# Attention in two heads at a time: row-tiled score products in place of stacked ones, padded blocks of v, one chain for the decays

## The chip, the cores and the metric

The kernel runs on 1 core of one Trainium2 chip. A time is device microseconds (us) of that core for one execution. The kernel before takes 1095.51 us, the median of 3 runs (1094.81 to 1099.94).

## The reference

32 heads (4 batches of 8) of 576 positions by 64 features go through an attention with a forgetting decay, and what comes out, 2304 tokens of 512 features, goes through two feed-forward blocks. All is float32.

```
scores = scale * q @ k.T                     # scale = 1/8
cum    = cumsum(log(clip(f, 1e-4, 1)))       # along the 576 positions of a head
scores = where(causal, -1e9, scores + cum[:, None] - cum[None, :])
attn   = softmax(scores);  out = attn @ v
h = x @ w_in;    y = (max(h, 0) + log1p(exp(-abs(h)))) @ w_out
z = ((1 / (1 + exp(-(y @ w_gate)))) * (y @ w_val)) @ w2_out
```

## The kernel before, in words

Matrix products are made of float32r operands (one pass through TensorE, with fewer bits than float32). To keep the precision every operand is split in a high part (the value cast to float32r) and a low part (the rest), and a product is high·high + high·low + low·high. Small pieces are multiplied in float32 instead, which stands in a trace as two MATMUL records for one instruction.

The attention works on 16 pairs of heads. The 576 queries of a head are four blocks of 128 and a rest of 64. A pair has nine score tiles, `t` = 0 to 3 (blocks of head 0), 4 (the rests of both heads in one tile of 128 rows) and 8 down to 5 (blocks of head 1), of the causal widths `W9`: 128, 256, 384, 512 and 576.

- `scores` (lines 236 to 265): `X` holds the high part of q on rows 0 to 63 and its low part on rows 64 to 127, `Y` the high part of k twice, so that one product over 128 rows (K = 128) makes two of the three terms. `X2` holds the high part of q again and two rows of ones, `Y2` the low part of k and the two rows of the decay, so that a second product with K = 66 makes the third term and the decay. That is two products a tile (line 262; line 251 for tile 4). The first block of a head (tiles 0 and 8) is made of a product with K = 2 for the decay (line 258, rows 64 and 65) and a float32 product with K = 64 (line 259). A score tile lies in PSUM under tag `s` (two buffers), tile 4 under tag `X`.
- `minimum` (VectorE, line 269) adds the causal mask, scales, writes the tile to SBUF (`P`) and finds the row's extreme; `exp` (ScalarE, line 274) follows.
- `transposes` (TensorE, line 291, 25 blocks of 128 by 128 a pair) put the tiles of `P` into PSUM tag `t` (two buffers); `evac_h` (ScalarE) and `evac_l` (VectorE, line 310) take the high and the low part out. The blocks listed as "f" in `GROUPS` stay float32 and are copied once (`evac_f`).
- `pv` multiplies with v: line 371 in float32r with the high and low parts of v side by side (128 columns of weights), line 367 in float32 for the "f" blocks, some of them with 64 columns of weights. The sums stand in PSUM tags `Y` (head 0) and `X` (head 1).
- `out_a` (ScalarE) and `out_b` (VectorE, line 386) add the two halves, `out_c` (GpSimd) divides by the row sums, `out_d` stores to `xT`.
- The splits of q, k and v into parts are casts and subtractions on GpSimd, VectorE and ScalarE (`copy` line 193 to 197, `sub` line 201).

The order of the work is written out: `run` sorts all operations of all pairs by 9·p + `WHEN[op]` (`START` for pair 0, `END` for pair 15), mixed with steps of the first feed-forward block (`TICKS`, `LATE_TICKS`, `X_STEPS`, `UNITS`), and every engine takes its instructions strictly in that order. Pairs overlap: while pair p makes scores, pair p-1 is transposed and multiplied with v. At the start `begin` follows the list `BEGIN`: clip, logarithm, running sum and the two parts of the decay are made first for head 0, then for head 1, then for all 32 heads (into `nb_d` in DRAM, from which later pairs fetch theirs). During and after the attention VectorE, ScalarE and GpSimd also unpack the weights of the feed-forward blocks; TensorE runs these blocks from about 227 us to the end. None of that code changes.

Of the kernel before, what the change touches and what calls it, by code (L numbers as in the profile page):

```python
# [21 lines left out]
class Attention:  # L22


    S = 576
# [10 lines left out]
    def pools(self, pool, io_pool):  # L36
# [10 lines left out]

    BEGIN = [["clip", 0], ["clip", 1], ["ones", 0], ["log", 0], ["scan", 0], ["m"], ["log", 1], ["mask4"],
             ["mask"], ["qh", 0, "A"], ["scan", 1], ["ql", 0, "P"], ["kh", 1, "A"], ["high", 0],
             ["kh", 0, "P"], ["high", 1], ["ahead"], ["kl", 0, "P"], ["kl", 1, "P"], ["clip", 2], ["log", 2],  # L50
             ["low", 1], ["ones", 1], ["qh", 1, "A"], ["low", 0], ["scan", 2], ["q2", 0, "A"], ["high", 2],
             ["ql", 1, "P"], ["low", 2], ["q2", 1, "A"]]

    def begin(self, ahead):

        nc, S = self.nc, self.S
        R = 2 * self.NP
        c = self.pp.tile([128, sum(self.W9)], F32, tag="P", name="decays")  # L60
        f0, cum0 = c[64:66, 0:2 * S], c[64:66, 2 * S:4 * S]
        fs, cums = [c[0:R, 0:S]], [c[0:R, S:2 * S]]
        nb = c[0:R, 2 * S:4 * S].rearrange("p (t s) -> p t s", t=2).bitcast(F32R)
        nc.sync.dma_start(f0, bass.AP(self.f.tensor, self.f.offset, [[0, 2], [1, 2 * S]]))
        P0 = self.R[0] = {}
        self.load_q(P0, 0)
        self.load_k(P0, 0)
        nc.sync.dma_start(fs[0], self.f)
        self.load_first(P0, 0)
        fs = [f0[:, 0:S], f0[:, S:]] + fs  # L70
        cums = [cum0[:, 0:S], cum0[:, S:]] + cums
        self.constants()
        X, X2, Y, Y2 = (self.buf(P0, 0, n) for n in ("X", "X2", "Y", "Y2"))
        qr, kr = P0["qr"], P0["kr"]
        m = self.c.tile([128, 1], F32, name="m")
        self.nb = self.dr.tile([R, 2, S], F32, name="nb_d")

        def op(n, h=0, e="V"):
            f, cum = fs[h], cums[h]
            h = min(h, 1)  # L80
            if n == "ahead":
                ahead()
            elif n == "m":
                nc.gpsimd.memset(m[64:66], 1.0)
                nc.gpsimd.memset(m[64:65], 0.0)
            elif n == "mask":
                nc.gpsimd.memset(self.mask, 0.0)
                nc.gpsimd.affine_select(self.mask, self.mask, pattern=[[-1, 512]], compare_op=ALU.is_ge,
                                        fill=-8e9, base=384, channel_multiplier=1)
            elif n == "mask4":  # L90
                nc.gpsimd.memset(self.mask4, 0.0)
                for i in range(2):
                    M = self.mask4[64 * i:64 * i + 64]
                    nc.gpsimd.affine_select(M, M, pattern=[[-1, S]], compare_op=ALU.is_ge, fill=-8e9, base=512,
                                            channel_multiplier=1)
            elif n == "ones":
                nc.gpsimd.memset(self.fix[h][64:96].bitcast(F32), 1.0)
            elif n == "clip":
                nc.vector.tensor_scalar(f, f, 1e-4, 1.0, op0=ALU.max, op1=ALU.min)
            elif n == "log":  # L100
                nc.scalar.activation(f, f, AF.Ln)
            elif n == "scan":
                nc.vector.tensor_tensor_scan(cum, f, f, 0.0, op0=ALU.add, op1=ALU.bypass)
            elif n == "high" and f is not fs[2]:
                nc.vector.tensor_scalar(f.bitcast(F32R), cum, -8.0, m[64:66], op0=ALU.mult, op1=ALU.mult)
            elif n == "high":
                nc.vector.tensor_scalar(nb[:, 0], cum, -8.0, None, op0=ALU.mult)
            elif n == "low" and f is not fs[2]:
                nc.vector.scalar_tensor_tensor(Y2[64:66, h], cum, -8.0, f, op0=ALU.mult, op1=ALU.subtract)
            elif n == "low":  # L110
                nc.vector.scalar_tensor_tensor(nb[:, 1], cum, -8.0, nb[:, 0], op0=ALU.mult, op1=ALU.subtract)
                nc.sync.dma_start(self.nb, nb.bitcast(F32))
            elif n == "qh":
                self.copy(None, X[0:64, h, 128:], qr[:, h, 128:], e)
            elif n == "ql":
                self.sub(None, X[64:128, h, 128:], qr[:, h, 128:], X[0:64, h, 128:], e)
            elif n == "q2":
                self.copy(None, X2[0:64, h, 128:], X[0:64, h, 128:], e)
            elif n == "kh":
                self.copy(None, Y[:, h], kr[:, h], e)  # L120
            elif n == "kl":
                self.sub(None, Y2[0:64, h], kr[0:64, h], Y[0:64, h], e)
        for o in self.BEGIN:
            op(*o)

    def constants(self):

        c, S = self.c, self.S
        self.mask = c.tile([128, 512], F32, name="mask")
        self.mask4 = c.tile([128, S], F32, name="mask4")  # L130
        self.fix = [c.tile([128, 2, S], F32R, name=f"X2_{i}") for i in range(2)]

    def constants2(self):
        nc, c = self.nc, self.c
# [6 lines left out]
        self.vr = [c.tile([128, 1024], F32, name=f"vr{i}") for i in range(self.NVR)]  # L141
        for t in self.vr:
            for o in (0, 192):
                nc.gpsimd.memset(t[:, o:o + 64], 0.0)
        self.pta = [[c.tile([128, 896], F32R, name=f"PTa{w}{i}") for w in "hl"] for i in range(2)]
        self.ptb = [c.tile([128, 1536], F32R, name=f"PTb{w}") for w in "hl"]
        self.ptf = [c.tile([128, 768], F32, name=f"PTf{i}") for i in range(2)]
# [3 lines left out]

    def load_q(self, R, p):
        b, hp = divmod(p, self.HP)
        R["qr"] = self.io.tile([64, 2, self.S], F32, tag="qr", bufs=1, name=f"qr{p}")
        self.nc.sync.dma_start(R["qr"], self.q[b, hp])

    def load_k(self, R, p):
        b, hp = divmod(p, self.HP)
        kr = R["kr"] = self.io.tile([128, 2, self.S], F32, tag="kr", bufs=1, name=f"kr{p}")
        for i in range(2):  # L160
            self.nc.sync.dma_start(kr[64 * i:64 * i + 64], self.k[b, hp])

    def load_first(self, R, p):

        b, hp = divmod(p, self.HP)
        for n, x in (("q0", self.q), ("k0", self.k)):
            R[n] = self.io.tile([64, 2, 128], F32, tag=n, name=f"{n}_{p}")
            self.nc.sync.dma_start(R[n], x[b, hp][:, :, 0:128])

    def load_v(self, R, p):  # L170
# [6 lines left out]
        else:  # L177
            nc.sync.dma_start(V[:, 0:4], rows[0:512].rearrange("(j p) e -> p j e", p=128))
            nc.sync.dma_start(V[0:64, 4], rows[512:576])

    def buf(self, R, p, n):
        if n == "X2":
            return self.fix[p % 2]
# [732 lines left out]
```

## Time and profile before

| | |
|---|---|
| median of 3 runs | 1095.51 us (1094.81 to 1099.94) |
| profiled execution | 1094.54 us, of which the span from the first to the last instruction is 1092.5 us |
| mean granted TensorE clock | 0.997 |
| TensorE (PE) | 1060.6 us busy, 97% of the span |
| VectorE (DVE) | 526.0 us, 48% |
| ScalarE (ACT) | 427.9 us, 39% |
| GpSimd (POOL) | 173.3 us, 16% |
| chain that ended last | PE 90%, DVE 5%, DMA 2%, ACT 1%, issue 1% |

A busy share is a mean over stages with different limits: the profile has to be read by stretches. A MATMUL record is longer than the time that it occupies TensorE, because matmuls are pipelined. What one costs is read from the start of one record to the start of the next. PEld are the loads of weights (the stationary operand), which run beside the matmul before them.

### The profile page before, as it was taken

The page shows a single profiled execution, that of the slowest core. Times are in us where ns is not written, and L with a number is a line of the kernel's source. Part 1 is how long each engine was busy: PE and PEld are TensorE (multiplying, and loading weights), DVE is VectorE, ACT ScalarE, POOL GpSimd, SP SyncE. Part 2 cuts the span into 40 slices and gives each one's busy share as a digit, 9 for nine tenths or more (in the row PEclk, how much of TensorE's full clock was granted, in tenths as well). Part 3 has the DMA queues.
Part 4 walks back from the last instruction along what each step waited for, and adds up shares of the span by engine and source line. Part 5 has one row for each costly group of instructions (what it writes and reads, how often), then busy time and mean ns, then how long its engine had stood idle before and what let it go on. Part 6 is the DMA issues. An engine that isn't in the chain of part 4 may idle for free.

```text
span 1092.5 us, 14676 instructions
## 1 busy us (share of the span) xinstructions
PE 1060.6 (97%) x5512; PEld 947.4 (87%) x5512; DVE 526.0 (48%) x1098; ACT 427.9 (39%) x930; POOL 173.3 (16%) x195
## 2 busy tenths in 40 slices
PE   3899999989999999999999999999999999999998
PEld 2777777767889999999999999999999999999997
DVE  8899989898971211212117879622222222222212
ACT  3788888865652222222225655311111111111111
POOL 7777777651000000000000000000000000000000
PEclk9999999999999999999999999999999999999999
DMA  6767766555531010010003544110010100100000
GB/s 184 180 161 185 187 173 163 153 156 173 210 143 56 17 36 15 18 43 9 17 35 119 181 167 171 53 42 17 1 44 16 37 15 8 37 15 8 30 1 29
DMA packets 52676, 90.26 MB, mean 83 GB/s; under 512 B 6704, under 2 KB 34304, under 8 KB 52606
## 3 DMA queue, kind: packets, MB, share of 16 engines
q1 hardware_dynamic: 52606, 89.33, 27.6%
q8 instruction: 43, 0.70, 0.3%
q14 instruction: 27, 0.22, 0.1%
HBM read 71.49 MB, written 14.38 MB: 79 GB/s over the span
## 4 chain that ended last, share of the span: by engine, by line
PE 90%; DVE 5%; DMA 2%; ACT 1%; issue 1%; SPq 0%; ACTq 0%
PE h L603 5%; PE h L604 5%; PE h L602 5%; PE pg L604 5%; PE pg L602 5%; PE pg L603 5%; PE pv L602 5%; PE pv L604 5%; PE pv L603 5%; PE t L291 4%; PE x L371 3%; PE s L262 3%; PE zX L753 3%; PE zX L752 3%; PE zX L751 3%; PE x L367 3%
## 5 line engine op out<-in xcount | busy, mean ns | idle before, releaser
L723 DVE TENSOR_TENSOR sg<-pv,sg 128x384 f32<-128x384 f32 x72 | 40.1, 557 | 262.0 <-PE pv L604 261.7
L644 DVE TENSOR_TENSOR gl<-L,gh 128x448 fp32r<-128x448 f32 (+1 forms) x80 | 51.0, 637 | 223.5 <-ACT gh L643 215.0
L632 ACT ACTIVATE L<-h 128x448 f32<-128x448 f32 (+1 forms) x80 | 44.3, 554 | 195.9 <-PE h L604 195.7
L603 PE MATMUL h<-xl,wi_h 128*128 128x448 f32 (+1 forms) x320 | 118.5, 370 | 1.0 <-POOL xl L595 1.0
L602 PE MATMUL h<-xh,wi_h 128*128 128x448 f32 (+1 forms) x320 | 118.7, 371 | 0.4 <-DVE xh L594 0.4
L604 PE MATMUL h<-xh,wi_l 128*128 128x448 f32 (+1 forms) x320 | 118.4, 370 | 0.0
L722 ACT ACTIVATE sg<-pg 128x384 f32<-128x384 f32 x72 | 35.3, 491 | 180.8 <-PE pg L604 180.8
L604 PE MATMUL pg<-yh,wg_l 128*128 128x384 f32 x288 | 97.1, 337 | 0.0
L602 PE MATMUL pg<-yh,wg_h 128*128 128x384 f32 x288 | 97.0, 337 | 0.0
L603 PE MATMUL pg<-yl,wg_h 128*128 128x384 f32 x288 | 96.7, 336 | 0.0
L735 ACT CAST qh<-sg 128x384 fp32r<-128x384 f32 x72 | 36.9, 512 | 151.8 <-DVE sg L723 151.8
L602 PE MATMUL pv<-yh,wv_h 128*128 128x384 f32 x288 | 96.2, 334 | 0.0
L603 PE MATMUL pv<-yl,wv_h 128*128 128x384 f32 x288 | 96.2, 334 | 0.0
L604 PE MATMUL pv<-yh,wv_l 128*128 128x384 f32 x264 | 88.2, 334 | 0.0
L274 ACT ACTIVATE P<-P,m 128x256 f32<-128x256 f32 (+2 forms) x144 | 83.4, 581 | 2.0 <-DVE m L269 1.6
L269 DVE CUSTOM_DVE_ANT_0 P<-s,mask 128x512 f32<-128x512 f32 (+3 forms) x144 | 72.3, 513 | 11.2 <-PE s L262 5.6
L603 PEld LDWEIGHTS h<-xl,wi_h 128*128 128x128 f32 x320 | 60.2, 188 | 7.6 <-POOL xl L595 1.3
L602 PEld LDWEIGHTS h<-xh,wi_h 128*128 128x128 f32 x320 | 60.2, 188 | 7.4 <-DVE xh L594 0.8
L604 PEld LDWEIGHTS h<-xh,wi_l 128*128 128x128 f32 x320 | 60.1, 188 | 6.3
L291 PE MATMUL t<-ident,P 128*128 128x128 f32 x400 | 63.1, 283 | 1.0 <-DVE PTbl L310 0.7
L262 PE MATMUL s<-Y,X 128*128 128x256 f32 (+2 forms) x192 | 58.0, 388 | 2.8 <-DVE m L269 2.8
L736 DVE TENSOR_TENSOR ql<-sg,qh 128x384 fp32r<-128x384 f32 x72 | 40.4, 561 | 42.1 <-ACT qh L735 42.1
(159 smaller groups left out, 2406.5 us busy)
## 6 DMA issues: line engine op xcount, KB each, us to landing
kr<-in_k_dram SPq DMA_DIRECT2D x32, 288.0 KB
raw_wi<-in_moe_w_in_dram SPq DMA_DIRECT2D x16, 512.0 KB
raw_wo<-in_moe_w_out_dram SPq DMA_DIRECT2D x16, 512.0 KB
raw_wg<-in_moe_w_gate_dram SPq DMA_DIRECT2D x12, 512.0 KB
raw_wv<-in_moe_w_val_dram SPq DMA_DIRECT2D x12, 512.0 KB
raw_w<-in_moe_w_out_dram SPq DMA_DIRECT2D x12, 512.0 KB
vr<-in_v_dram SPq DMA_DIRECT2D x15, 320.0 KB
qr<-in_q_dram SPq DMA_DIRECT2D x16, 288.0 KB
```

The lines of the kernel that those rows point to most:

```text
L262: nc.tensor.matmul(ps[:, 0:w], L[0:K, h, 128 * i:128 * i + 128], Rr[0:K, h, 0:w], start=K == 128, stop=K != 128)
L269: self.nc.vector.tensor_tensor_reduce(P, src, mask, -0.125, 3e38, op0=ALU.add, op1=ALU.min, accum_out=R["m"][:, t:t + 1])
L274: self.nc.scalar.activation(P, P, AF.Exp, bias=R["m"][:, t:t + 1], scale=-1.0, accum_out=R["sum"][:, t:t + 1])
L291: nc.tensor.transpose(ps[:, 128 * n:128 * n + 128], R["P"][:, o:o + 128], self.ident)
L602: nc.tensor.matmul(ps, ah, bh, start=start and i == 0, stop=False)
L603: nc.tensor.matmul(ps, ah, bl, start=False, stop=False)
L604: nc.tensor.matmul(ps, al, bh, start=False, stop=stop and i == n - 1)
L632: nc.scalar.activation(g, ph, AF.Softplus)
L644: nc.vector.tensor_sub(gl, s, gh)
L723: nc.vector.tensor_mul(s, pv, s)
L735: nc.scalar.copy(gh, s)
L736: nc.vector.tensor_sub(gl, s, gh)
```

## The change

`before.py` becomes `after.py`; only the class `Attention` changes.

- **Scores.** Head 0 lies on partitions 0 to 63 and head 1 on 64 to 127, in `Xh`, `Xl`, `Yh`, `Yl` (high and low parts of q and k). Blocks i = 0 to 3 of both heads are made together in a round of eight products: three terms and the decay (`one` times `nb`), each once with K = 64 on the upper and once on the lower half of the array, the halves taking turns, into two PSUM tiles (both buffers of tag `s`). The first block is made 256 wide, of which 128 are used. Tile 4 is made of eight products with K = 128 over the block-shaped rest of q.
- **Products with v.** All 25 blocks are split in high and low parts and multiplied in float32r with 128 columns of weights; blocks of zeros in `PTb` fill pieces up to 256 wide.
- **Loads and splits.** No second copies of k and q, no separate loads of the first blocks; q is loaded in three pieces, v and the decays in two. All splits run on GpSimd for all pairs but the first, whose casts are ScalarE's.
- **Start.** One chain of clip, logarithm, sum and the two parts over 66 partitions serves head 0, all heads and head 1 at once; the list `BEGIN` is gone. The tables `WHEN`, `START` and `END` are new; `TICKS`, `LATE_TICKS`, `X_STEPS` and `UNITS` stay.

```diff
     def begin(self, ahead):
...
+        f, cum = c[0:66, 0:S], c[0:66, S:2 * S]
+        row = lambda h, n: bass.AP(self.f.tensor, self.f.offset + S * h, [[0, n], [1, S]])
+        nc.sync.dma_start(c[0:32, 0:S], row(0, 32))
+        nc.sync.dma_start(c[32:64, 0:S], self.f)
+        nc.sync.dma_start(c[64:66, 0:S], row(1, 2))
...
+        nc.vector.tensor_scalar(f, f, 1e-4, 1.0, op0=ALU.max, op1=ALU.min)
+        nc.scalar.activation(f, f, AF.Ln)
+        self.copy(None, self.buf(P0, 0, "Xh", 640), P0["qr"], "A")
+        self.copy(None, self.buf(P0, 0, "Yh", S), P0["kr"], "A")
+        nc.vector.tensor_tensor_scan(cum, f, f, 0.0, op0=ALU.add, op1=ALU.bypass)
+        nc.vector.tensor_scalar(hi, cum, -8.0, m[0:66], op0=ALU.mult, op1=ALU.mult)
+        nc.vector.scalar_tensor_tensor(lo, cum, -8.0, f, op0=ALU.mult, op1=ALU.subtract)
+        nc.sync.dma_start(self.nb[:, 0], c[32:64, 0:S])
+        nc.sync.dma_start(self.nb[:, 1], lo[32:64].bitcast(F32))
+        ahead()
+        self.ql(P0, 0)
+        self.kl(P0, 0)
+        self.constants2()
...
+    def v_high(self, R, p):
+
+        R["V"] = self.vp.tile([128, 5, 2, 2, 64], F32R, tag="V", name=f"V{p}")
+        self.copy(("v_high",), R["V"][:, :, :, 0], R["vr"].rearrange("p j (h e) -> p j h e", h=2))
...
+        n = 4
+        if i == 4:
             ps = self.ps.tile([128, 1024], F32, tag="X", name=f"s{p}_4")
-            for h, q0, M in ((1, 448, 128), (0, 512, 64)):
-                for L, Rr, K in ((X, Y, 128), (X2, Y2, 66)):
-                    for c in range(2):
-                        nc.tensor.matmul(ps[0:M, 224 + 288 * c:512 + 288 * c], L[0:K, h, q0:q0 + M],
-                                         Rr[0:K, h, 288 * c:288 * c + 288], start=K == 128, stop=K != 128)
...
-            if i == 0:
-                nc.tensor.matmul(ps[:, 0:192], X2[64:66, h, 0:128], Y2[64:66, h, 0:192], start=True, stop=False)
-                nc.tensor.matmul(ps[:, 0:128], R["q0"][:, h], R["k0"][:, h], start=False, stop=True)
-            else:
-                for L, Rr, K in ((X, Y, 128), (X2, Y2, 66)):
-                    nc.tensor.matmul(ps[:, 0:w], L[0:K, h, 128 * i:128 * i + 128], Rr[0:K, h, 0:w],
-                                     start=K == 128, stop=K != 128)
...
+            for c in range(2):
+                for j, (L, r) in enumerate(((Xh[:, 512:640], Yh), (Xl[:, 512:640], Yh), (Xh[:, 512:640], Yl),
+                                            (self.one[:, 128:256], nb))):
+                    nc.tensor.matmul(ps[:, 224 + 288 * c:512 + 288 * c], L, r[:, 288 * c:288 * c + 288],
+                                     start=j == 0, stop=j == n - 1)
...
+        w = self.W9[i]
+        N = max(w, 256)
+        ps = [self.ps.tile([128, 512], F32, tag="s", bufs=2, name=f"s{p}_{i}_{h}") for h in range(2)]
+        q = slice(128 * i, 128 * i + 128)
+        for j, (L, r) in enumerate(((Xh[:, q], Yh), (Xl[:, q], Yh), (Xh[:, q], Yl), (self.one[:, 0:128], nb))):
+            for h in range(2):
+                o = slice(64 * h, 64 * h + 64)
+                nc.tensor.matmul(ps[h][:, 0:N], L[o], r[o, 0:N], start=j == 0, stop=j == n - 1)
...
+    PV = [[[("a", 0, 0, 256), ("a", 256, 256, 320)], [("b", 768, 0, 256), ("b", 1024, 256, 320)],
+           [("b", 0, 256, 320)], [("b", 1856, 320, 256)], [("b", 640, 512, 64)]],
+          [[("a", 576, 0, 320), ("a", 896, 320, 256)], [("b", 1344, 0, 320), ("b", 1664, 320, 256)],
+           [("b", 320, 0, 320)], [("b", 2112, 0, 256)], [("b", 704, 0, 64)]]]
...
-            nc.tensor.matmul(acc, v, self.pt(p, tile, 0)[0:K, col:col + n], start=j == 5, stop=j == 5)
...
+        v = R["V"][:, j, h].rearrange("p a e -> p (a e)")
+        for w in range(2):
+            for tile, col, x, n in self.PV[h][j]:
...
-    ENGINE = {("evac_f", 5): "A", ("evac_f", 6): "V", ("k_high", 1): "V", ("q_high", 0): "V", ("q_high", 1): "A"}
+    ENGINE = {}
...
+    END = {("rinv_d",): 19, ("out_c",): 26, ("out_d",): 27}
```

What the new tables make of the order is shown at three places. The first is TensorE in the attention's steady part, from the first blocks and the third block of pair 8 (tiles `s8_0`, `s8_8`, `s8_2`) to the tile after. Before:

```order
L258 MATMUL s8_0_1577<-Y2_8_1345,X2_0_109 128x192
L259 MATMUL s8_0_1577<-k0_8_1358,q0_8_1356 128x128
L371 MATMUL x7_0_1580<-PTah1_179,V7_1461 128x448
L371 MATMUL x7_0_1580<-PTal1_180,V7_1461 128x448
L367 MATMUL x7_0_1580<-PTf1_184,vr1_169 128x128
L258 MATMUL s8_8_1587<-Y2_8_1345,X2_0_109 128x192
L259 MATMUL s8_8_1587<-k0_8_1358,q0_8_1356 128x128
L291 MATMUL t7_6_1593<-ident_163,P7_1279 128x128 x3
L262 MATMUL s8_2_1599<-Y_8_1350,X_8_1371 128x384
L262 MATMUL s8_2_1599<-Y2_8_1345,X2_0_109 128x384
L291 MATMUL t7_4_1605<-ident_163,P7_1279 128x128 x4
```

Now the third blocks of both heads (pair 7 here, tiles `s7_2_0` and `s7_2_1`) are one round of eight:

```order
L220 MATMUL s7_2_0_1590<-Yh_7_1296,Xh_7_1304 128x384
L220 MATMUL s7_2_1_1591<-Yh_7_1296,Xh_7_1304 128x384
L220 MATMUL s7_2_0_1590<-Yh_7_1296,Xl_7_1385 128x384
L220 MATMUL s7_2_1_1591<-Yh_7_1296,Xl_7_1385 128x384
L220 MATMUL s7_2_0_1590<-Yl_7_1349,Xh_7_1304 128x384
L220 MATMUL s7_2_1_1591<-Yl_7_1349,Xh_7_1304 128x384
L220 MATMUL s7_2_0_1590<-nb1_106,one_108 128x384
L220 MATMUL s7_2_1_1591<-nb1_106,one_108 128x384
```

Two products a tile, one tile at a time, have become eight that alternate between the halves of the array and fill both buffers of `s` together; a pair has four such rounds. The second place is VectorE in the steady part of the changed kernel, from pair 5's first blocks (`s5_0_0`, `s5_0_1`) to its third (`s5_2_0`, `s5_2_1`); `xs` is the result of pair 3 and `PTbl` a low part of pair 4.

```order
L227 ISA P5_1033,m5_1034<-s5_0_0_1160,mask_114 128x128
L227 ISA m5_1034 128x1
L227 ISA P5_1033,m5_1034<-s5_0_1_1161,mask_114 128x128
L227 ISA m5_1034 128x1
L337 TENSOR_TENSOR xs3_1141<-x3_1_1083,bs3_1142 64x576
L272 TENSOR_TENSOR PTbl_176<-t4_4_1180,PTbh_175 128x384
L227 ISA P5_1033,m5_1034<-s5_2_0_1208,mask_114 128x384
L227 ISA m5_1034 128x1
L227 ISA P5_1033,m5_1034<-s5_2_1_1209,mask_114 128x384
L227 ISA m5_1034 128x1
```

The minima of the two heads now stand directly one behind the other, where before other work and tiles lay between them. The third place is VectorE at the very start. Before:

```order
L99 TENSOR_SCALAR decays_95<-decays_95 2x576 x2
L103 SCALAR_TENSOR_TENSOR decays_95<-decays_95 2x576 x2
L105 TENSOR_SCALAR decays_95<-decays_95,m_114 2x576 x2
L99 TENSOR_SCALAR decays_95<-decays_95 32x576
L109 SCALAR_TENSOR_TENSOR Y2_0_113<-decays_95 2x576 x2
L103 SCALAR_TENSOR_TENSOR decays_95<-decays_95 32x576
L107 TENSOR_SCALAR decays_95<-decays_95 32x576
L111 SCALAR_TENSOR_TENSOR decays_95<-decays_95 32x576
L269 ISA P0_185,m0_186<-s0_1_196,mask_107 128x256
```

And now:

```order
L68 TENSOR_SCALAR decays_95<-decays_95 66x576
L72 SCALAR_TENSOR_TENSOR decays_95<-decays_95 66x576
L73 TENSOR_SCALAR decays_95<-decays_95,m_126 66x576
L74 SCALAR_TENSOR_TENSOR nb0_105<-decays_95 66x576
L227 ISA P0_194,m0_195<-s0_1_0_197,mask_114 128x256
```

Twelve instructions ahead of the first minimum have become four. On SyncE's queue the stores of `nb_d` stood behind the first three loads of weights, and now stand ahead of them.

## Rows read from the trace of the kernel before

**Rows 1.** Stretches: us, busy us (count) of PE, PEld, DVE, ACT, POOL; clock, DMA share.

```profile
0.00:27.00 27.00, 8.37 (x24) 6.10 (x24) 23.69 (x33) 10.28 (x19) 19.36 (x31) 1.00 0.66 184
58.19:206.22 148.03, 148.03 (x914) 117.76 (x913) 133.43 (x373) 127.22 (x349) 108.14 (x120) 1.00 0.71 175
210.00:260.00 50.00, 44.84 (x214) 33.87 (x215) 42.20 (x70) 31.38 (x64) 21.63 (x19) 0.97 0.46 143
```

**Rows 2.** VectorE's groups, 58.19 to 206.22 us; the x12 are twelve pairs.

```profile
L310 DVE TENSOR_TENSOR PTbl<-t,PTbh 128x512 fp32r<-128x512 f32 x24 | 16.3, 681 | 0.0
L197 DVE CAST X<-qr 64x448 fp32r<-64x448 f32 x12 | 15.1, 1257 | 1.0 <-DMA qr<-in_q_dram 1.0
L269 DVE CUSTOM_DVE_ANT_0 P<-s,mask 128x384 f32<-128x384 f32 x24 | 13.3, 553 | 0.4
...
L197 DVE CAST Y<-kr 128x576 fp32r<-128x576 f32 x12 | 5.4, 450 | 0.0
```

**Rows 3.** Timeline of TensorE: start us, us, engine, line, operation.

```profile
122.56 0.36 PE L371 MATMUL x<-PTal,V 128*128 128x448 f32 x1
122.76 0.31 PE L371 MATMUL x<-PTbh,V 128*128 128x320 f32 x1
122.91 0.31 PE L371 MATMUL x<-PTbl,V 128*128 128x320 f32 x1
...
124.96 1.09 PE L291 MATMUL t<-ident,P 128*128 128x128 f32 x8
125.81 0.45 PE L371 MATMUL x<-PTbh,V 128*128 128x448 f32 x1
...
127.19 0.35 PE L258 MATMUL s<-Y,X 2*128 2x192 f32 x1
127.47 0.48 PE L259 MATMUL s<-k,q 64*128 64x128 f32 x2
127.89 0.47 PE L371 MATMUL x<-PTah,V 128*128 128x448 f32 x1
128.20 0.37 PE L371 MATMUL x<-PTal,V 128*128 128x448 f32 x1
...
131.06 1.21 PE L251 MATMUL s<-Y,X 128*128 128x288 f32 x8
132.21 0.79 PE L367 MATMUL x<-PTf,vr 64*64 64x64 f32 x4
```

**Rows 4.** Loads of weights, 58.19 to 206.22 us: rows*columns, count, mean ns.

```profile
L262 PEld LDWEIGHTS s<-Y,X 66*128 66x128 f32 x72 | 13.7, 190 | 0.2
...
L258 PEld LDWEIGHTS s<-Y,X 2*128 2x128 f32 x24 | 4.3, 181 | 2.9
...
L251 PEld LDWEIGHTS s<-Y,X 128*64 128x64 f32 x24 | 3.2, 136 | 0.0
```

**Rows 5.** Timeline of the start, all engines.

```profile
2.46 1.29 DVE L99 TENSOR_SCALAR decays<-decays 2x576 f32<-2x576 f32 x2 [2.46 <-DMA decays<-in_f_dram]
...
8.96 3.05 POOL L201 TENSOR_TENSOR Y<-kr,Y 64x576 fp32r<-64x576 f32 x2
9.21 1.53 DVE L99 TENSOR_SCALAR decays<-decays 32x576 f32<-32x576 f32 x1
10.77 4.05 DVE L109 SCALAR_TENSOR_TENSOR Y<-decays 2x576 fp32r<-2x576 f32 x2
10.78 0.68 ACT L101 ACTIVATE decays<-decays 32x576 f32<-32x576 f32 x1 [2.71 <-DVE decays L99]
...
14.85 1.35 DVE L103 TENSOR_TENSOR_SCAN decays<-decays 32x576 f32<-32x576 f32 x1
...
14.97 0.49 PE L258 MATMUL s<-Y,X 2*128 2x192 f32 x1 [14.97 <-DVE Y L109]
...
16.23 0.45 DVE L107 TENSOR_SCALAR decays<-decays 32x576 fp32r<-32x576 f32 x1
...
16.71 0.75 DVE L111 SCALAR_TENSOR_TENSOR decays<-decays 32x576 fp32r<-32x576 f32 x1
```

More of the change, by code (lines that the diff above doesn't have):

```diff
@@ L45 @@
     O9 = [sum([128, 256, 384, 512, 576, 512, 384, 256, 128][:i]) for i in range(9)]
[L48 to L52, printed above, removed]
@@ L72, in begin @@
-        self.constants()
-        X, X2, Y, Y2 = (self.buf(P0, 0, n) for n in ("X", "X2", "Y", "Y2"))
-        qr, kr = P0["qr"], P0["kr"]
-        m = self.c.tile([128, 1], F32, name="m")
[L76 to L122, printed above, removed]
@@ new lines, in begin @@
+        ahead()
+        self.ql(P0, 0)
+        self.kl(P0, 0)
+        self.constants2()
+    def constants(self):
+        nc, c, S = self.nc, self.c, self.S
+        self.qrs = [c.tile([128, 640], F32, name=f"qr{i}") for i in range(2)]
+        for q in self.qrs:
+            nc.gpsimd.memset(q[0:64, 576:640], 0.0)
+            nc.gpsimd.memset(q[64:128, 512:576], 0.0)
+        self.nbs = [c.tile([128, S], F32R, name=f"nb{i}") for i in range(2)]
+        nc.gpsimd.memset(self.nbs[0][64:128].bitcast(F32), 0.0)
+        self.one = c.tile([128, 256], F32R, name="one")
+        o = self.one[:].bitcast(F32)
+        nc.gpsimd.memset(o, 0.0)
+        for r, t in ((0, 128), (64, 192)):
+            nc.gpsimd.memset(o[r:r + 2, 0:128], 1.0)
+            nc.gpsimd.memset(o[r:r + 2, t:t + 64], 1.0)
@@ L129, in constants @@
         self.mask = c.tile([128, 512], F32, name="mask")
+        nc.gpsimd.memset(self.mask, 0.0)
+        nc.gpsimd.affine_select(self.mask, self.mask, pattern=[[-1, 512]], compare_op=ALU.is_ge,
+                                fill=-8e9, base=384, channel_multiplier=1)
         self.mask4 = c.tile([128, S], F32, name="mask4")
-        self.fix = [c.tile([128, 2, S], F32R, name=f"X2_{i}") for i in range(2)]
     def constants2(self):
-        nc, c = self.nc, self.c
+        nc, c, S = self.nc, self.c, self.S
@@ L135, in constants2 @@
+        nc.gpsimd.memset(self.mask4, 0.0)
+        for i in range(2):
+            M = self.mask4[64 * i:64 * i + 64]
+            nc.gpsimd.affine_select(M, M, pattern=[[-1, S]], compare_op=ALU.is_ge, fill=-8e9, base=512,
+                                    channel_multiplier=1)
+        nc.gpsimd.memset(self.nbs[1][:].bitcast(F32), 0.0)
         ident = c.tile([128, 128], F32, name="ident")
@@ L232, in v_low, with kh, kl @@
-    def v_low(self, R, p, h):
-        V, Vr = self.v_parts(R, p)
-        self.sub(("v_low", h), V[:, :, 2 * h + 1], Vr[:, :, h], V[:, :, 2 * h])
-    def scores(self, R, p, t):
+        for h in range(2):
+            self.nc.sync.dma_start(self.nbs[p % 2][64 * h:64 * h + 2].bitcast(F32), self.nb[2 * p + h])
+    def kh(self, R, p):
+        self.copy(("kh",), self.buf(R, p, "Yh", self.S), R["kr"])
+    def kl(self, R, p):
+        self.sub(("kl",), self.buf(R, p, "Yl", self.S), R["kr"], R["Yh"])
```

252 lines of the change are left out of this document (87 added, 165 removed), and 6 rows, old and new, of tables (START, WHEN).

## The prediction

> **What bounds the kernel now.** I first cut the run into stretches. In 148.03 us of steady attention TensorE is busy for 148.03 us [rows 1]. Twelve pairs pass in it (a cast done once a pair stands there 12 times [rows 2]), so a pair takes 12.34 us, of which VectorE works 11.1, ScalarE 10.6 and GpSimd 9.0. TensorE is the bound with no gap, the other three have 1.2 to 3.3 us of slack a pair, and the DMA engines are busy for 0.71 of the time. The start is different: in the first 27 us TensorE works 8.4 us and VectorE 23.7. In the handover, 210 to 260 us, TensorE lacks 5.2 us of 50 [rows 1]. After it TensorE runs the feed-forward blocks, which do not change. So three terms are wanted: what a pair costs on TensorE, the start, the handover.
>
> For the first I read TensorE's timeline from start to start [rows 3]. A product 448 wide is followed by the next after 0.20 us and one 320 wide after 0.15, so 128 columns cost 0.05 us and the widths 256, 384 and 512 cost 0.125, 0.175 and 0.225. Eight transposes take 0.85 us, 0.106 each. Tile 4's eight products take 1.15 up to the next group, about 1.1 without the pause that ends them.
>
> Two more prices matter. A load of weights with 128 columns is 54 ns longer than one with 64 (190 against 136 ns [rows 4]), so 128 columns occupy the load path for about 0.108 us, however few rows they have (66 rows 190 ns, 2 rows 181 ns). It hides beside a product of 256 columns or more, but not at a change of the array's shape: the first product after the float32 one with 64 rows is followed only after 0.31 us, where the same width costs 0.20 elsewhere [rows 3]. The 2-row product before it shows the rest. It takes 0.28 us: 0.108 of load and 0.075 for 192 columns leave about 0.095, in which the array drains. A change of shape costs 0.095 + 0.108 = 0.20 us.
>
> **The change on TensorE, part by part, for one pair.** Unchanged: 25 transposes, 25 x 0.106 = 2.66; tile 4, eight products of the same width, 1.1; the transpose of the sums, 0.1. Removed: the stacked products of blocks 1 to 3, 4 x (0.125 + 0.175 + 0.225) = 2.1; the first blocks, 2 x (0.28 + 0.42) with a drain ahead of each, 1.6; the float32r products with v, 8 x 0.20 + 4 x 0.15 = 2.2. What is left of 12.34 is 2.6 us, the float32 products with v and their changes of shape, removed too.
>
> Added with v: 12 products 256 wide, 12 of 320 and 4 of 64 (these at the price of a load), 12 x 0.125 + 12 x 0.15 + 4 x 0.108 = 3.7 in place of 4.8, all in one shape. Everything but the score rounds then comes to 7.6 us, and the rounds decide: the pair breaks even if four of them cost 4.75.
>
> A round is eight products of 64 rows. It pays the change of shape on entry and on exit, 0.095 + 0.108 twice, 1.6 us for four rounds. For what lies between, the trace shows no two row tiles at work together, so I bound it. If the halves overlap fully, loads too, four terms cost one width each: 4 x (0.125 + 0.125 + 0.175 + 0.225) = 2.6, and the rounds 4.2. If they do not overlap at all, 5.2 and 6.8. Between these lies the case that products overlap but loads of weights follow each other: eight loads, 0.86 us, the last product's width, two drains and the load of the next group, 4 x (0.095 + 0.864 + 0.095 + 0.108) + 0.65 = 5.3. I take this: the nearest rows are those of rows 4, where a load costs its 128 columns whether it fills 2 rows or 66, so 64-row loads should be no cheaper, and 0.108 is as long as a 256-wide product. The pair then costs 7.6 + 5.3 = 12.9 us, 0.55 more than before.
>
> The Trainium skill, TensorEngine Tiling (Array Packing), under Key Properties, says that "Different tiles can execute LdWeights and Matmul in parallel". By that rule the rounds cost 4.2 us a pair and the pair 11.8; no run here shows two tiles at work, and it is rival A below.
>
> **The other engines.** VectorE loses the casts of q and k, 1.26 + 0.45 us a pair [rows 2], and a copy of 256 columns, and gains 768 columns of low parts, at 0.68 us for 512 [rows 2] about 1.0: it falls to 10 us or so. ScalarE loses a cast of 448 columns and gains 256 columns of high parts, about the same. GpSimd takes all splits, but on full partitions: counted over its casts, subtractions and the division 4288 columns a pair in place of 3968, some 9.7 us by its present rate. SyncE issues about one load more a pair and half as many bytes of k. None of them reaches 12.9, so I cost them at nothing; in rival A they have 1 us or so of cover left. A round does fill both score buffers, so the next one waits for two minima that stand one behind the other; by the prices above TensorE has 1.3 us of other work or more between rounds, and the two widest minima that are due so soon cost 2 x 0.55 [rows 2]. I take 0 for that and bound it at 0.5 us a pair.
>
> Fifteen pairs (the first one's scores belong to the start) make 15 x 0.55 = +8.3 us; the bounds are 15 x -0.53 = -8 and 15 x 2.06 = +31.
>
> **The start.** Now VectorE begins at 2.46 us and TensorE at 14.97, released by the low part of the decay [rows 5]; head 0's and head 1's instructions stand apart, with the clip for all heads between. One chain over 66 partitions costs what the chain over 32 does: clip 1.53, logarithm 0.68, sum 1.35, parts 0.45 and 0.75, together 4.8 us [rows 5]. f comes by three loads, by my estimate a microsecond later, and operations beside GpSimd can take twice as long (the two low parts took 4.05 for two, 2.0 each against 0.75). That puts the decay at 8.5 to 11 us. GpSimd's two subtractions, 1.5 us each at the rate of rows 5, end about then too, and weights now load behind the stores of the decay. I take -5 us, and bound it at -9 (VectorE's later casts of q and k fall away here too) and +2 (the first weights come late and VectorE waits for them).
>
> **The handover.** The feed-forward steps keep their places, and the last pair's order has three entries of its own. The products with v of the last pair now all stand ahead of the first feed-forward unit, with nothing else for TensorE beside the last low parts. I take +3 us, between -3 and +10.
>
> Sum: 1094.5 us of the profiled execution + 8.3 - 5 + 3 = 1101; the median of the runs lies 1.0 above that execution, so 1102.
>
> **Rivals.**
> A. Full overlap, loads too: the pair falls to 11.8, and waits on minima can give back up to half of it. 1095.5 - 8 - 5 + 3 = 1085 to 1090, not slower than before. For it speaks that the two halves read different partitions and write different buffers; against it, that no row shows any overlap. It decides as soon as a round costs less than 1.2 us.
> B. No overlap of the halves, or hardly any: 14.4 us a pair, 1095.5 + 31 - 5 + 3 = 1124. For it: every product of before starts only when the one ahead has streamed.
> C. The rounds cost as forecast, but the double use of the score buffers stalls each pair for 0.3 to 0.5 us, or the handover loses its 10: 1107 to 1110. For it: 11 of 12.34 us of VectorE are taken now, and its order is strict.
>
> **How the numbers follow.** I give the forecast 0.40, A 0.25, B 0.25, C 0.10. The range is 1084 to 1124, from A to B; the forecast's own is 1096 to 1109. A measurement of this kernel tells 0.5%, 5.5 us, from no change. The forecast lies at +6.5, so within it slower has 0.55, the same 0.35, faster 0.10; in A faster 0.75, same 0.20, slower 0.05; B is slower, and C nearly always. That makes faster 0.23, same 0.20, slower 0.57.
>
> **What would show it.** On TensorE's timeline of the changed kernel, the starts inside a round: about 0.11 us apart at every width is the forecast; pairs of starts close together and one width to the next pair is A; a width apart each time is B. A round's 0.2 us at either end shows the change of shape, and the period of tile 4 shows the pair: 12.9, 11.8 or 14.4. The first product should start at 9 to 11 us. I am wrong if TensorE is not busy throughout the steady part, or if the start moves by less than 3 us.

## The result and the profile after

The changed kernel takes 1086.18 us (median of 5 runs, 1085.06 to 1088.03) against 1096.39 us of the kernel before on the same chip: ratio 0.9903, 95% interval 0.9878 to 0.9928. It is about 1% faster, where 0.6% slower was forecast. The time lies inside the range, near its lower end, and between the two times given for rival A, which had a chance of 0.25. Its profiled execution took 1085.96 us, 8.6 less than that of before.

The stretches of the kernel after, with the columns of [rows 1]; the second runs from tile 4 of pair 2 to tile 4 of pair 15, thirteen pairs:

```profile
0.00:27.00 27.00, 10.80 (x44) 7.73 (x45) 16.07 (x33) 12.91 (x29) 19.48 (x43) 0.98 0.78 213
39.74:190.79 151.05, 151.05 (x1225) 128.44 (x1224) 136.36 (x391) 133.78 (x377) 101.39 (x90) 1.00 0.42 119
...
205.00:210.00 5.00, 4.23 (x21) 3.49 (x18) 2.76 (x9) 3.20 (x11) 3.02 (x3) 0.50 0.61 166
```

TensorE is still busy without a gap in the steady part, but a pair takes 151.05 / 13 = 11.62 us in place of 12.34. The other engines' shares of a pair are 10.5 (VectorE), 10.3 (ScalarE) and 7.8 us (GpSimd). Where the 8.4 us between the two spans arise is read from three landmarks: tile 4 of pair 2 starts 4.9 us earlier than before (39.74 against 44.61 us), tile 4 of pair 15 14.3 us earlier (190.79 against 205.08), and the feed-forward blocks from unit 16 on 8.5 us earlier (482.41 against 490.91 us at the same product). So the start gives 4.9, thirteen pairs give 9.4, and the handover takes 5.8 back.

A round of scores and its neighbours on TensorE, after, to be held against [rows 3]:

```profile
128.63 0.43 PE L322 MATMUL x<-PTbh,V 128*128 128x320 f32 x2
128.89 0.42 PE L322 MATMUL x<-PTbl,V 128*128 128x320 f32 x2
129.24 0.39 PE L220 MATMUL s<-Yh,Xh 64*128 64x256 f32 x2
129.46 0.28 PE L220 MATMUL s<-Yh,Xl 64*128 64x256 f32 x2
129.58 0.28 PE L220 MATMUL s<-Yl,Xh 64*128 64x256 f32 x2
129.70 0.28 PE L220 MATMUL s<-nb,one 64*128 64x256 f32 x2
129.91 0.53 PE L322 MATMUL x<-PTah,V 128*128 128x256 f32 x2
130.28 0.43 PE L322 MATMUL x<-PTal,V 128*128 128x256 f32 x2
130.54 0.93 PE L250 MATMUL t<-ident,P 128*128 128x128 f32 x7
131.40 0.44 PE L220 MATMUL s<-Yh,Xh 64*128 64x384 f32 x2
131.68 0.34 PE L220 MATMUL s<-Yh,Xl 64*128 64x384 f32 x2
131.86 0.34 PE L220 MATMUL s<-Yl,Xh 64*128 64x384 f32 x2
132.03 0.34 PE L220 MATMUL s<-nb,one 64*128 64x384 f32 x2
132.30 0.30 PE L322 MATMUL x<-PTbh,V 128*128 128x64 f32 x1
```

Each row of a round is a pair of products, one per head ("x2"). From row to row there is one width (0.12 us for 256 columns, 0.17 to 0.18 for 384), not two widths and not two loads; only the first step of a round is longer (0.22 and 0.28 us), behind the change of shape. The loads of weights show the same:

```profile
129.24 0.19 PEld L220 LDWEIGHTS s<-Yh,Xh 64*128 64x128 f32 x2 [0.16 <-issue]
129.35 0.19 PEld L220 LDWEIGHTS s<-Yh,Xl 64*128 64x128 f32 x2
129.47 0.19 PEld L220 LDWEIGHTS s<-Yl,Xh 64*128 64x128 f32 x2
```

One load still lasts as long as in [rows 4] (0.19 us), and two start every 0.12 us. The start of the kernel after, for [rows 5]:

```profile
3.31 0.59 DVE L68 TENSOR_SCALAR decays<-decays 66x576 f32<-66x576 f32 x1 [3.31 <-DMA decays<-in_f_dram]
4.65 1.35 DVE L72 TENSOR_TENSOR_SCAN decays<-decays 66x576 f32<-66x576 f32 x1 [0.75 <-ACT decays L69]
...
6.66 2.06 DVE L74 SCALAR_TENSOR_TENSOR nb<-decays 66x576 fp32r<-66x576 f32 x1
...
8.17 0.58 PE L220 MATMUL s<-Yh,Xh 64*128 64x256 f32 x2 [8.17 <-ACT Yh L162]
```

One chain of 66 rows is done at 8.72 us, and TensorE starts at 8.17 in place of 14.97, since the first terms of a round need no decay.

### The profile page after: what moved, and what is told of

It is laid out like the page before. It is cut to its first block, busy times and chain, and to the rows that moved or that the text cites. A ratio compares the mean times of both kernels' runs of the same rounds, so it can differ in the third digit from the quotient of the medians.

```text
span 1084.1 us, 15094 instructions
## 1 busy us (share of the span) xinstructions
PE 1052.2 (97%) x5800; PEld 950.2 (88%) x5800; DVE 504.5 (47%) x1076; ACT 421.4 (39%) x926; POOL 155.3 (14%) x158
## 4 chain that ended last, share of the span: by engine, by line
PE 89%; DVE 3%; DMA 3%; issue 1%; SPq 1%; ACT 1%; POOL 0%; DVEq 0%; ACTq 0%; POOLq 0%
PE h L513 5%; PE h L514 5%; PE h L512 5%; PE x L322 5%; PE pg L514 5%; PE pg L512 5%; PE pg L513 5%; PE pv L512 5%; PE pv L513 5%; PE pv L514 5%; PE s L220 4%; PE t L250 4%; PE zX L663 3%; PE zX L662 3%; PE zX L661 3%; PE oY L513 2%
## 5 line engine op out<-in xcount | busy, mean ns | idle before, releaser
L232 ACT ACTIVATE P<-P,m 128x128 f32<-128x128 f32 (+4 forms) x144 | 83.6, 585 | 9.1 <-DVE m L227 8.8
L227 DVE CUSTOM_DVE_ANT_0 P<-s,mask 128x256 f32<-128x256 f32 (+3 forms) x144 | 69.7, 508 | 11.4 <-PE s L220 8.9
L663 PE MATMUL zX<-w_h,ql 128*128 128x512 f32 x144 | 57.2, 397 | 0.0
```

The costliest lines, as they stand in the source:

```text
L227: self.nc.vector.tensor_tensor_reduce(P, src, mask, -0.125, 3e38, op0=ALU.add, op1=ALU.min, accum_out=R["m"][:, t:t + 1])
L232: self.nc.scalar.activation(P, P, AF.Exp, bias=R["m"][:, t:t + 1], scale=-1.0, accum_out=R["sum"][:, t:t + 1])
L663: nc.tensor.matmul(a, block(gl, b), wh, start=False, stop=last)
```

## The experiments

Each starts from the changed kernel unless it says otherwise. Times are medians; ratios are to the kernel before, with 95% intervals. Runs 2, 5, 8 and 9 were made on another chip than the rest: the kernel before takes 1099.81 us there, and 1095.23 to 1096.64 us where the others ran.

**1. Halves apart in the program.** The order of the loops is swapped, so that head 0's four products are issued first.

```
-        for j, (L, r) in enumerate(((Xh[:, q], Yh), ...)):
-            for h in range(2):
+        for h in range(2):
+            for j, (L, r) in enumerate(((Xh[:, q], Yh), ...)):
```

> Starts from the changed kernel; in the four score rounds head 0's four products now stand ahead of head 1's four, so that only the last product of the one half and the first of the other can run together. Theory (the gain comes from two halves that load and stream at the same time): a round streams seven widths instead of four, 3 x (0.125 + 0.125 + 0.175 + 0.225) = 1.95 us more a pair, 15 pairs, +29 us: about 1115 us, the pair 11.6 -> 13.5 us. Rival 1 (the halves gain nothing from each other, the gain comes from the products with v alone): no change, within 3 us of 1086. Rival 2 (what I forecast: the loads of weights follow each other and set the round): also no change, since eight loads follow each other in either order.

Measured: 1090.32 us, ratio 0.9942 (0.9922 to 0.9962), pair 12.0 us. That is neither 1115 nor 1086. TensorE's timeline of this run, a round 512 wide and one 256 wide:

```profile
125.64 0.51 PE L220 MATMUL s<-Yh,Xh 64*128 64x512 f32 x2
...
130.33 0.38 PE L220 MATMUL s<-Yh,Xh 64*128 64x256 f32 x1
130.55 0.28 PE L220 MATMUL s<-Yh,Xl 64*128 64x256 f32 x1
130.67 0.28 PE L220 MATMUL s<-Yl,Xh 64*128 64x256 f32 x1
130.69 0.38 PE L220 MATMUL s<-Yh,Xh 64*128 64x256 f32 x1
130.79 0.27 PE L220 MATMUL s<-nb,one 64*128 64x256 f32 x1
```

There is one product Yh,Xh per head and round. In the wide round both start together, though three other products stand between them in the program; in the narrow one head 1's first product starts before head 0's fourth. So the two halves do not keep the program's order between them, and my experiment did not take the overlap away. The second half starts 0.36 us late in that narrow round because its score buffer is not free. VectorE in the same stretch:

```profile
128.68 1.16 DVE L278 TENSOR_SCALAR r<-sum 128x9 f32<-128x9 f32 x1
...
130.00 0.63 DVE L227 CUSTOM_DVE_ANT_0 P<-s,mask 128x512 f32<-128x512 f32 x1
```

The minimum that reads the buffer ends at 130.63 us, and head 1's first product starts at 130.69, 0.06 us behind that end, as in every pair of this run. The minimum comes late since `r<-sum`, which stands ahead of it in VectorE's order, lasts 1.16 us here and 0.81 us in the changed kernel. The wait, 0.36 us, is nearly all of the 0.38 us that the pair grew; the swapped order itself costs next to nothing. It does not show as idle time of TensorE, since the other half is at work. The next run takes the overlap away in another manner.

**2. Both heads on one half.**

```
-                o = slice(64 * h, 64 * h + 64)
+                o = slice(0, 64)
```

> The order of the two halves in a round did not matter, so this takes the second half of the rows away instead: the changed kernel with both heads' products of the four score rounds on rows 0 to 63 (the second head's scores are then computed from the first head's q and k, which is the part of the computation that changes). Same instructions, widths and waits. Theory (two halves of the array draw their loads and products side by side): without a second half a round streams eight widths instead of four, 4 x (0.125 + 0.125 + 0.175 + 0.225) = 2.6 us more a pair, less what waits for minima hid: the pair 11.6 -> 14.0 to 14.2 and the time 1086 + 15 x 2.5 = 1123 (1115 to 1130). Rival (the halves gain nothing, the time of a round is loads that follow each other): no change, within 3 us of 1086.

Measured: 1127.58 us, ratio 1.0277 (1.0243 to 1.0311). Tile 4 starts at 60.74 and, twelve pairs later, at 232.01 us: a pair takes 14.27 us. The same round there:

```profile
127.40 0.50 PE L220 MATMUL s<-Yh,Xh 64*128 64x256 f32 x2
127.74 0.40 PE L220 MATMUL s<-Yh,Xl 64*128 64x256 f32 x2
127.98 0.40 PE L220 MATMUL s<-Yl,Xh 64*128 64x256 f32 x2
```

Two products now take two widths (0.24 us). The second half is worth 14.27 - 11.62 = 2.65 us a pair, as the widths say (2.6). Without it the change would be slower, at the price that rival B named (14.4).

**3. New scores with the old products with v.** `load_v`, `v_high`, `v_low`, `GROUPS`, `PV`, `pv` and the evacuations with their places come from the kernel before.

> The changed kernel with the products with v of the kernel before: its float32 products, its V over three blocks, its transposed tiles and its order for them; the score rounds, the start and the splits of q and k are those of the changed kernel. Theory (the score rounds cost 4.1 us a pair in place of 3.7, and the products with v give the gain, 3.7 in place of 4.8 us): the pair is 11.6 + 1.1 = 12.7 us, 0.4 above before, and the time 1086 + 15 x 1.1 = 1102, between 1096 and 1108 by the handover. Rival (the row-tiled rounds are themselves the gain): the pair is 11.9 or less and the time 1091 or less.

Measured: 1097.05 us, ratio 1.0005 (0.9989 to 1.0022). Tile 4 runs from 51.59 to 203.19 us in twelve pairs, 12.63 a pair. So the new scores with the old products with v cost 0.29 us a pair (12.34 to 12.63), and the new products with v bring 1.02 (12.63 to 11.62). Not all of that is their price on TensorE, for this run's rounds wait for score buffers. The widest round, and VectorE ahead of it:

```profile
127.75 0.42 DVE L169 COPY PTf<-t 128x256 f32<-128x256 f32 x1
...
128.29 0.55 DVE L238 CUSTOM_DVE_ANT_0 P<-s,mask 128x384 f32<-128x384 f32 x1
...
128.61 0.78 PE L231 MATMUL s<-Yh,Xh 64*128 64x512 f32 x2
```

The row of the first two products lasts 0.78 us, where it lasts 0.50 in the changed kernel: head 1's product starts 0.28 us behind head 0's, 0.06 us after the end of the minimum that frees its buffer, and ahead of that minimum stands a copy that belongs to the old products with v. In the round 384 wide the second half is 0.19 us late. The two rounds take 1.40 and 1.09 us, in the changed kernel 1.12 and 0.90. Without these 0.47 us the pair would be about 12.16 us (an estimate): the scores alone would then be 0.18 us cheaper than before, and the new products with v would give 0.54. Over the whole run the scores alone win the start and lose it again in the pairs and the handover.

**4 and 5. New products with v in the kernel before.** The opposite split, tried twice: `load_v`, `V`, `GROUPS`, `PV`, `pv` and the evacuations with their places from the changed kernel, in the kernel before.

```
-    NVR = 3
+    NVR = 2          # second try: 1
-            R[n] = self.io.tile([64, 2, 128], F32, tag=n, name=f"{n}_{p}")
+            R[n] = self.io.tile([64, 2, 128], F32, tag=n, bufs=1, name=f"{n}_{p}")   # first try only
```

> The kernel before with the products with v of the changed one: float32r over five blocks with zeros, its transposed tiles and its order for them; scores, decays, start and the splits of q and k stay as before. Two buffers for v in place of three and one for the first blocks of q and k in place of two, loaded later, make room. Theory: TensorE's pair falls by 1.1 us to 11.25, but VectorE, 11.1 us a pair before, gets 768 columns of low parts more (+1.0) and loses a copy of 256 columns (-0.4), 11.7 us: VectorE becomes the bound, the pair is 11.7 to 12.1, and the time 1096 - 15 x (0.25 to 0.65) = 1086 to 1092. Rival (TensorE stays the bound, VectorE's load does not matter): pair 11.25 and 1080. Rival (the padded products gain nothing alone): 1094 to 1098.

> As the run before of the new products with v in the kernel before, but with two buffers again for the first blocks of q and k, loaded where the kernel before loads them, and one buffer for v: in the earlier run SyncE waited for TensorE to free the single one, and 16.3 us a pair came of that queue, not of the products. Theory: TensorE alone would need 12.34 - 1.02 = 11.3 us a pair (1.02 is what the old products with v cost in the changed kernel, 12.63 against 11.61), VectorE has 11.1 + 1.0 - 0.4 = 11.7, so the pair is 11.7 to 12.1 and the time 1086 to 1092. Rival (VectorE's load does not matter): pair 11.3, about 1081. If a queue still holds the pair above 12.3, the run says nothing of the products.

Measured: 1155.97 us (ratio 1.0542, 1.0505 to 1.0579) and 1162.64 us (1.0570, 1.0543 to 1.0597). Neither prices the products: TensorE was busy for only 41 of 50 us and no other engine was full. SyncE's waits of the two runs, 60 to 200 us (waiting line, releaser, us in total, times, longest):

```profile
SPq L215 <- DVE X L192: 45.5, 9, 9.8
```

```profile
SPq L215 <- DVE X L192: 23.5, 9, 5.1
SPq L174 <- POOL V L196: 23.1, 9, 3.2
```

Loads stand behind others that wait, in an order put together from two kernels. Whether the new products with v need VectorE's relief stays open; run 7 tries it from the other side.

**6. First blocks 128 columns wide.**

```
-        N = max(w, 256)
+        N = w
```

> The changed kernel with the round of the first blocks 128 columns wide instead of 256. Theory (a load of weights of 128 columns costs 0.108 us and the two halves load at the same time): the pairs of products in that round stand 0.11 us apart instead of 0.125, at most 0.06 us a pair, no change that can be measured (1084 to 1088). If the two loads followed each other, the round would keep eight starts 0.11 us apart and be no faster either; the spacing inside the round on TensorE's timeline tells these apart. Rival (columns alone are paid): 4 x 0.063 = 0.25 us a pair, -4 us.

Measured: 1086.71 us, ratio 0.9904 (0.9870 to 0.9937): no change that the times show. A pair takes 11.52 us, against 11.61 over the same twelve pairs of the changed kernel, a little more than the 0.06 us that were expected at most; 0.08 of it lie in that round (0.59 us in place of 0.67):

```profile
128.70 0.33 PE L220 MATMUL s<-Yh,Xh 64*128 64x128 f32 x2
128.86 0.28 PE L220 MATMUL s<-Yh,Xl 64*128 64x128 f32 x2
128.98 0.27 PE L220 MATMUL s<-Yl,Xh 64*128 64x128 f32 x2
129.09 0.27 PE L220 MATMUL s<-nb,one 64*128 64x128 f32 x2
```

Behind the first step (0.16 us in place of 0.22) the steps stay at 0.11 to 0.12 us with half the columns: a load sets the step, and it is one load's length for two loads. Loads that follow each other would give 0.22.

**7. Casts of q and k on VectorE.**

```
-    ENGINE = {}
+    ENGINE = {("kh",): "V", ("qh",): "V"}
```

> The changed kernel with the high parts of q and k cast by VectorE (128 x 640 and 128 x 576 columns a pair) instead of GpSimd, about the work that VectorE had before and lost. Theory (the new products with v load VectorE with 768 columns more, and the pair of 11.6 us is only reached because the full-height casts went to GpSimd): VectorE goes from about 10.5 to 11.5 us a pair and its strict order stalls TensorE, pair 11.8 to 12.3, time 1089 to 1097. Rival (VectorE's load does not matter while it is below TensorE's): pair 11.6, within 2 us of 1086.

Measured: 1094.12 us, ratio 0.9974 (0.9957 to 0.9991). The sum was right and its place wrong. A pair takes 11.77 us (47.05 to 200.01 us in thirteen), only 0.15 more; but tile 4 of pair 2 starts at 47.05 us instead of 39.74. VectorE takes its casts in order, and in the start the first one waits for its DMA:

```profile
18.21 0.46 DVE L164 CAST Yh<-kr 128x576 fp32r<-128x576 f32 x1 [5.04 <-DMA kr<-in_k_dram]
```

Behind it stand the minima for which TensorE then waits 10.5 us. In the steady part VectorE's busy time hardly rises (89.9 us of 100 after, 90.4 here, 60 to 160 us, or 10.4 and 10.6 us a pair), although the two casts take 0.92 us a pair (437 and 487 ns), for another operation became shorter: `r<-sum` takes 810 ns after and 163 ns here. It is not GpSimd's casts that make it long, but its subtraction for the low part of k (`Yl<-kr,Yh`): after, `r<-sum` starts some 0.65 us into that subtraction and ends some 0.03 us behind it; here GpSimd is idle at that time. Run 11, in which the casts are GpSimd's, has both lengths in one trace:

```profile
68.79 0.15 DVE L278 TENSOR_SCALAR r<-sum 128x9 f32<-128x9 f32 x1
...
79.95 1.59 POOL L168 TENSOR_TENSOR Yl<-kr,Yh 128x576 fp32r<-128x576 f32 x1
80.79 0.79 DVE L278 TENSOR_SCALAR r<-sum 128x9 f32<-128x9 f32 x1
```

GpSimd has nothing to do at 68.79 us. So VectorE's load was not raised by the 0.92 us that were meant, and neither the theory nor its rival was put to the test in the steady part. The 0.15 us a pair arise in one round, as in run 1:

```profile
134.77 0.68 DVE L227 CUSTOM_DVE_ANT_0 P<-s,mask 128x512 f32<-128x512 f32 x1
...
135.34 0.56 PE L220 MATMUL s<-Yh,Xh 64*128 64x256 f32 x2
```

Head 1's first product starts 0.18 us behind head 0's, again 0.06 us after the minimum has ended; in the changed kernel's steady pairs it is at most 0.03 us behind.

**8. Stores of the outputs earlier.**

```
-("out_d",): 40.0472
+("out_d",): 39.4
```

> The changed kernel with the store of a pair's output 0.65 steps earlier, so that the store of pair 11 stands ahead of the second load of the feed-forward input on SyncE's queue, not behind it. Theory (that load waits for GpSimd at 195 to 197 us, holds the store up, the store holds the output buffer, and VectorE and TensorE wait for that at 201 to 204 us, after which the granted clock falls to 0.50): TensorE's wait of 2.5 us at 202 us goes and the dip in the clock with it, -3 to -4 us, 1082 to 1083. Rival (VectorE sets the handover and the time is lost a few us later anyway): within 1 us of 1086.

Measured: 1083.02 us, ratio 0.9848 (0.9830 to 0.9866), clear of the changed kernel's interval, and 3.9 us under run 9, which leaves these stores in their place on the same chip. In the kernel after, SyncE's waits from 185 to 200 us (columns as in run 4) begin with

```profile
SPq L498 <- POOL xl L505: 6.9, 1, 6.9
```

and the timeline shows the load, the store behind it, VectorE's idle time behind the store and TensorE's behind that:

```profile
197.16 0.34 SPq L498 DMA_DIRECT2D xr<-xT  x1
197.54 0.47 SPq L347 DMA_DIRECT2D xT<-xs  x1
...
201.19 0.75 DVE L337 TENSOR_TENSOR xs<-x,bs 64x576 f32<-64x576 f32 x1 [2.95 <-DMA xT<-xs]
...
202.09 0.50 PE L322 MATMUL x<-PTah,V 128*128 128x256 f32 x2 [2.52 <-DVE xs L337]
```

With the store ahead of that load, the stretches from 200 to 210 us read (columns as in [rows 1]):

```profile
200.00:205.00 5.00, 3.27 (x27) 2.60 (x26) 4.18 (x14) 3.82 (x14) 4.63 (x5) 1.00 0.43 126
205.00:210.00 5.00, 4.75 (x38) 4.26 (x38) 3.02 (x8) 4.15 (x12) 0.99 (x2) 1.00 0.69 193
```

The granted clock stays at 1.00 where it fell to 0.50, the lower of the two levels, after TensorE had waited; later in the handover it still dips in both (to 0.66 after, to 0.67 here, means of 5 us). From tile 4 of pair 15 to the feed-forward blocks (the product at 482.41 us after) it takes 288.1 us in place of 291.6; before took 285.8. So by these two traces 3.5 of the 5.8 us given back were SyncE's queue. Other runs put a bound on such a reading: those that leave the stores in their place take 291.6 to 292.2 us there (1, 6 and 7) and 289.5 (9), and run 3, whose stores stand where they did before the change and which has no such wait, takes 291.7 us by other waits.

**9. Decay rows earlier.**

```
-("decay_rows",): -2.9757
+("decay_rows",): -8.5
```

> The changed kernel with the load of a pair's decay rows 5.5 steps earlier, so that the one of pair 1 is issued ahead of two loads of weights and the loads of q, and lands before TensorE wants it at 26.69 us. Theory (TensorE waits 2.6 us there for that load alone): -2.0 to -2.6 us, about 1084. Rival (behind it stands another wait of the start, of VectorE's minima or of the splits of pair 1): within 1 us of 1086.

Measured: 1086.92 us, ratio 0.9880 (0.9860 to 0.9900): no gain, the rival holds. The wait at 26.69 us is gone, another one stands behind it, and tile 4 of pair 2 is even later (41.17 us):

```profile
31.82 0.66 PE L250 MATMUL t<-ident,P 128*128 128x128 f32 x4 [1.90 <-DVE PTal L272]
```

**10 and 11. Handover, and handover with start.**

```
-("out_d",): 40.0472
+("out_d",): 35.4
-LATE_TICKS = [8.53364, ...
+LATE_TICKS = [9.1, ...
-        N = max(w, 256)
+        N = w
# the second run also:
-("decay_rows",): -2.9757
+("decay_rows",): -8.5
-        others = [(t, W.tick) for t in TICKS] + ...
+        others += [one(t, W.LOAD) for t in (24, 33, 45, 60, 80, 100, 120)]
+            others += [one(b - 3, W.SCALE), one(b + .3, W.SHIFT), one(b + 9.3, W.LOW), one(b + 18.3, W.SIGN), ...
```

> The changed kernel with three small edits: the stores of the outputs at 35.4 instead of 40.05, so that those of pairs 11 to 13 all stand ahead of the feed-forward loads that wait; the first late step of weights at 9.1 instead of 8.53, behind the last low parts of the last pair, for which TensorE waits 1.9 us; the first blocks' round 128 columns wide. Theory (the handover lost its time to SyncE's queue and to this step on VectorE): -3 for the queue, -1.5 to -3 for the step, -1 for the round, 1078 to 1081. Rival (what is given back in one place is lost at the next, VectorE being full there): 1082 to 1084, no better than the earlier stores alone.

> As the run with the three edits of the handover, and in the start: the decay rows 5.5 steps earlier, four of the loads of weights out of the first 30 us, and the conversion of four blocks of weights spread one operation at a time over pairs 2 to 13, two of them out of the start and two out of the handover. Theory (the start is bound by the DMA engines and by VectorE, both of which convert and load weights there): tile 4 of pair 2 starts at 36 to 38 us instead of 39.7, the steady pair stays below 11.65, the handover has 5 us less of VectorE: 1072 to 1078. Rival (an operation inserted into VectorE's strict order stalls TensorE every pair, 0.2 to 0.5 us): 1080 to 1086.

Measured: 1080.77 us, ratio 0.9859 (0.9835 to 0.9883), and 1081.42 us, ratio 0.9854 (0.9829 to 0.9879). Both are faster than the kernel before, and their intervals end about where the changed kernel's begins (0.9878); by their ratios neither is better than the stores alone (0.9848), which were run on the other chip. In the trace of the first the handover takes 286.0 us, as short as before, and tile 4 of pair 15 starts at 189.44 us. In the second tile 4 of pair 2 starts at 40.19 us, no earlier; the pairs from there on take 11.7 to 12.3 us instead of 11.53, and the last of them 16.5 in the profiled execution, which at 1087.33 us is slower than the median; the handover falls to 283.2 us. Its rival was right: what the spread conversion frees in the handover it costs in the pairs.

## Why the prediction was wrong, step by step

**The step that failed** is the choice for the rounds: "products overlap but loads of weights follow each other", 5.3 us for four rounds. Loads of the two halves run at the same time: they start in pairs in the trace after, 0.12 us from pair to pair, a pair of 128-wide products still takes one load's length (run 6), and with one half only the rounds cost 2.65 us more (run 2). From the first product of each to the next group the four rounds take 3.4 us, and about 4.2 with what the changes of shape put on the products around them, where 5.3 were forecast. I had read [rows 4], where a load costs its 128 columns however few rows it fills, as saying that two loads with half the rows cost two. They say what one load costs, and nothing of two in different halves. The rule of the Trainium skill that I quoted (TensorEngine Tiling (Array Packing), Key Properties: "Different tiles can execute LdWeights and Matmul in parallel") is what the trace shows: the two products of a row start 3 to 30 ns apart, and two loads start every 0.12 us.

**What held.** By the same prices full overlap makes 4.2 us for the rounds and 11.8 for the pair; measured 11.62. The price of a change of shape was right: a round 256 wide takes 0.67 us (129.24 to 129.91), four widths of 0.12 and 0.19 more, and the pairs of products ahead of it and behind it take 0.35 and 0.37 us where others of their width take 0.26. That is 0.39 us for two changes; the sum had 0.41. The double use of the score buffers, taken at 0, costs 0.03 us a round at most, though in runs 1, 3 and 7 it cost 0.36, 0.47 and 0.18 us a pair.

How the 0.72 us that a pair gains divide between the products with v and the scores is not shown. By the prices, with full overlap, they are -1.1 and +0.5; run 3 as it stands gives -1.02 and +0.29, and without its waits -0.54 and -0.18. In each reading the change gains in its products with v; and with one half of the array a pair would be 1.9 us dearer than before. The float32 products that go, with their own changes of shape, are part of the first figure.

**The other engines at nothing** held in the steady part of the changed kernel, where TensorE is never idle. VectorE works 10.5 us a pair and not 10, of which 0.65 are what `r<-sum` takes longer beside GpSimd; GpSimd works 7.8 and not 9.7. But the cover of 1 us or so was not there where it counts: the minimum of a block 512 wide ends some 0.04 us before the round that takes its buffer starts, and in runs 1 and 7, where VectorE comes to it later, the pair is longer. What I did not see either is that the casts matter in the start, where they would cost 7.3 us (run 7).

**The start**, -5, came to -4.9 at pair 2, and that they agree is in part luck. The sum counts fifteen pairs and the landmarks thirteen; two more at 0.72 us are 1.4 us, which the measured start and handover hold. Counted as in the sum, fifteen pairs give -10.8 us in place of +8.3, and start and handover together +2.3 in place of -2. Within the start the first product is earlier than forecast (8.2 against 9 to 11 us). The 1.9 us between the 6.8 won there and the 4.9 left at pair 2 were not traced to one cause: run 9 took the one wait that showed and won nothing.

**The handover**, +3 between -3 and +10, came to +5.8, and of its cause the prediction had nothing: the store behind a waiting load on SyncE (3.5 us by two traces, run 8); the other 2.3 us were not traced. I had listed what stands in order on TensorE there, but not SyncE's queue, on which the stores of the outputs were moved from 37.58 to 40.05 steps.

By the landmarks the profiled execution adds up: 1094.5 - 9.4 - 4.9 + 5.8 = 1086.0. What stays open is what the new products with v would give in the kernel before, since TensorE stood idle for other reasons in both runs of that split.

## What to carry to other kernels

Price two row tiles as one: count a round by its widest product or one load, whichever is longer, plus 0.2 us at each change of shape, and do not add the loads of the halves. Then see that both halves find their buffers free: a wait of one half does not show as idle time of TensorE, but as a second start behind the first in a round. When a pair gets cheaper, look at what is issued in order behind a wait (SyncE's queue, VectorE's list) where one phase hands over to the next; a store moved by 0.65 steps gave back more than a third of what thirteen pairs had won. A test that reorders instructions does not take concurrency away between halves of the array; put both on the same rows.

## What was not expected of the hardware

The two halves of the array do not keep the program's order between them: in run 1 products of the second head started 14 ns after the first head's first one, past three of its others. A small VectorE operation (`r<-sum`, 128 x 9) that starts beside a subtraction of GpSimd ends only some 0.03 us after it: it lasts 0.81 us in the changed kernel, 1.16 us in run 1, where it starts earlier in the subtraction, and 0.16 us where GpSimd is idle. It stands ahead of the minimum that frees a score buffer, and so 0.35 us more of it made nearly all of what run 1 lost.
